# Modulation rows by matmuls of diagonals, and the second modulation part moved to the unit without PV

## The chip, the cores and the metric

The kernel runs on one core of a Trainium2 chip. A core has five engines, each with its own instruction queue: TensorE (PE, with its weight loads shown as PEld), VectorE (DVE), ScalarE (ACT), GpSimd (POOL) and SyncE (SP), which here issues nearly all DMAs. Engines wait for each other and for DMAs through semaphores. The metric is the device time of one execution in microseconds, the median of several runs.

## The reference

One transformer block of the adaptive-layernorm kind, in bf16, for 2048 rows x of width 512. From a condition vector c come six modulation vectors of 512 elements, and then an attention part and a gated MLP are applied, each with a layernorm ahead of it and a gate behind it:

```python
mod = (_silu(c) @ w_mod).reshape(c.shape[0], 6, 1, -1)
sa, ca, ga, sb, cb, gb = (mod[:, 0].copy(), ..., mod[:, 5].copy())
h = _layernorm(x, axis=-1) * (1 + ca) + sa
x = x + ga * _A_ref(h, A_k_cache, A_v_cache, A_wq, A_wo)
h = _layernorm(x, axis=-1) * (1 + cb) + sb
x = x + gb * _B_ref(h, B_w_in, B_w_sp, B_b_sp, B_w_out)
```

`_A_ref` is attention with 32 query heads in 8 groups of 4 over cached keys and values (2048 keys, head width 128), with its projections wq and wo. `_B_ref` is the gated MLP: gelu of h @ w_in, a layernorm of one half, a 2048 x 2048 mix over the rows (w_sp, b_sp), the product with the other half, and w_out.

The vectors ga and gb multiply along the width of a row. Where a tile has 128 rows of x on its partitions and the 512 columns along the free axis, ga is needed as a 128 x 512 tile in which every partition holds the same row (`ga_rows`, `gb_rows`). The matmuls that compute the modulation give it the other way: 128 elements on the partitions, four columns (`modc`).

## The kernel before

**Units.** The attention runs in 128 units (`it` in the main loop, `u` for the unit whose scores are computed): 8 groups times 16 tiles of 128 query rows, each unit with the 4 heads of its group. A unit has 8 slots. In each slot PE computes a 128 x 1024 tile of scores into one of two `s_ps` buffers in PSUM (two matmuls of 512 columns, in `qk`), and ACT takes its exponential into SBUF. In the same slot PE does an eighth of the product with the values (PV) of an earlier unit, and what else the schedule puts there. The order of all work is written out by hand (`manual_schedule`): `at(it, slot, fn)` puts a function at the head of a slot, and `fill[it, slot]` one behind PV.

**By columns and by rows.** Units 0 to 7, the last ones, and every third one between work by columns: the scores have the keys on the partitions (line 1030), the exponentials go straight into a tile `pT`, and PV of the unit runs in the next unit (line 1086). Two of three units from unit 8 (`TURN_A = 2 * CT`) on work by rows (line 1011): the scores have the queries on the partitions, ACT sums each row as it goes (line 1018), and each head's 128 x 2048 exponentials are turned by a DMA transpose on SP's queue (`turn_rows`, line 1050) into a stripe of `pT`. Their PV (line 1065) runs 2 or 3 units later (`LAGS = (2, 3, 1)`). Unit 8's PV is in unit 10, unit 9's in unit 12, unit 10's in unit 11, unit 11's in unit 13. So no PV falls into unit 9.

**Tiles for pT.** There are three: `pT0`, `pT1` and `wsp`. `homes` gives each unit the one that has been free longest. `wsp` first holds the second part of the modulation weights (`wmod_b`, 4 x 512 columns, loaded in unit 1), and counts as free from unit CT + 2 = 6.

**Other work in the slots.** The query projection of the next four units (`qproj`, line 947, 16 matmuls of 512 columns, four for each head, copied out of PSUM by DVE at line 958) is spread over the units before; `set_fill` places it, for block 3 two to a slot over unit 9, with the banks `misc` and `o_ps` in turn. The output projection of a unit (`wo_proj`, line 1143, four matmuls in slots 4 to 7) comes three units after its PV, into the banks `misc`; DVE adds it up (lines 1128 to 1136). A bank name has two buffers.

**The modulation.** A part (`mod_part`, line 857) is 16 matmuls with one column each, for 512 elements. sa and ca are computed ahead of unit 0. sb and cb come from `mod_cols_b` at slot 4 of unit 4, ga and gb from `mod_rows` at slot 4 of unit 5. `mod_rows` copies the four columns of each into `modc`, writes them from POOL's queue into a line in DRAM (line 1216), and reads the line back to all partitions (line 1217). POOL's queue holds the two pairs one behind the other, and the second of each pair waits for the first to land.

**Loads of group 1.** wq, v and wo of group 1 are issued on SP's queue in slot 2 of unit 6 and in slots 2 and 5 of unit 7 (lines 722, 730, 740). `ga_rows` is first used in the last group, `gb_rows` in the last stage.

Of the kernel before, what the change touches and what calls it, by code (L numbers as in the profile page):

```python
# [575 lines left out]
def kernel(  # L576
# [19 lines left out]
    nc = tc.nc  # L596
    _, S, D = A_x.shape
    _, HKV, SK, DH = A_k_cache.shape
    HQ = A_wq.shape[1] // DH
    REP = HQ // HKV  # L600
# [5 lines left out]
    NDT = D // P  # L606
# [3 lines left out]
    CT = 512 // P  # L610
    FC = _f_chunk(FH)
    NFHC = FH // FC
    NSLOT = NKT // 2
# [17 lines left out]
    fast = ctx.enter_context(ExitStack())  # L631
# [3 lines left out]
    psum = fast.enter_context(  # L635
        tc.tile_pool(name="psum", bufs=2, space=bass.MemoryType.PSUM)
    )
    dram = fast.enter_context(tc.tile_pool(name="dram", bufs=1, space=bass.MemoryType.DRAM))
    res = fast.enter_context(tc.tile_pool(name="res", bufs=1))
    stat = fast.enter_context(tc.tile_pool(name="stat", bufs=2))  # L640
    wspp = fast.enter_context(tc.tile_pool(name="wspp", bufs=1, side="right"))
# [6 lines left out]
    ga_rows = res.tile([P, D], FP32, name="ga_rows")  # L648
    gb_rows = res.tile([P, D], FP32, name="gb_rows")
    modc = res.tile([P, 6 * NDT], FP32, name="modc")  # L650
# [12 lines left out]
    wmod_b = wspp.tile([P, NDT * 4 * D], BF16, name="wsp")[:].rearrange(  # L663
        "p (k n) -> p k n", k=NDT
    )
    ident = res.tile([P, P], BF16, name="ident")
    ones_bf = res.tile([P, P], BF16, name="ones_bf")
    mean_bf = res.tile([P, P], BF16, name="mean_bf")

    def bank(name):  # L670
        return psum.tile([P, 512], FP32, name=name)
# [33 lines left out]
    for i in range(2):  # L705
        part = slice(i * D, (i + 1) * D)
# [13 lines left out]
    def load_wq(g, engine):  # L720
        wqs[g] = early.tile([P, NDT, REP * DH], BF16, name="wq_g")
        engine.dma_start(
            out=wqs[g][:], in_=wq_dram[:, :, g * REP * DH : (g + 1) * REP * DH]
        )

    def load_v(g):
        v1 = late.tile([P, NKT, DV], BF16, name="v1")
        nc.gpsimd.memset(v1[:, :, DH:DV], 1.0)
        if g > 0:
            nc.sync.dma_start(out=v1[:, :, 0:DH], in_=v_dram[:, g])  # L730
        else:
            nc.sync.dma_start(out=v1[:, 0 : NKT // 2, 0:DH], in_=v_rows)
            nc.sync.dma_start(
                out=v1[:, NKT // 2 : NKT, 0:DH], in_=v_dram[:, 0, NKT // 2 : NKT]
            )
        groups.setdefault(g, {})["v1"] = v1

    def load_wo(g, engine):
        wo_g = late.tile([P, REP, D], BF16, name="wo_g")
        engine.dma_start(out=wo_g[:], in_=wo_dram[:, g * REP : (g + 1) * REP, :])  # L740
        groups[g]["wo"] = wo_g

    def load_k(g):
        kT = early.tile([P, SK], BF16, name="kT")
        nc.sync.dma_start_transpose(out=kT[:], in_=A_k_cache[0, g])
        groups.setdefault(g, {})["kT"] = kT
# [106 lines left out]
    def mod_part(i, wmod, w0, mc_ps):  # L853

        for dt in range(NDT):
            for kt in range(NDT):
                nc.tensor.matmul(  # L857
                    mc_ps[:, i * NDT + dt : i * NDT + dt + 1],
                    lhsT=wmod[:, kt, w0 + dt * P : w0 + (dt + 1) * P],
                    rhs=sc_bf[:, kt : kt + 1],  # L860
                    start=(kt == 0),
                    stop=(kt == NDT - 1),
                )

    def mod_copy(first, mc_ps):
        c0 = first * NDT
        nc.vector.tensor_copy(out=modc[:, c0 : c0 + NDT], in_=mc_ps[:, 0:NDT])
        nc.vector.tensor_scalar_add(
            out=modc[:, c0 + NDT : c0 + 2 * NDT], in0=mc_ps[:, NDT : 2 * NDT], scalar1=1.0
        )  # L870
# [15 lines left out]
    mc_ps = bank("misc")  # L886
# [15 lines left out]
    for k in range(2):  # L902
        for dt in (2 * k, 2 * k + 1):
# [13 lines left out]
    for dt in range(NDT):  # L917
        if dt == 2:
            k_turn((0, 1, 2, 3), (nc.vector.tensor_copy, nc.scalar.copy))
        for hh in range(REP):  # L920
            nc.tensor.matmul(
                q_ps[hh // 2][:, hh % 2 * P : (hh % 2 + 1) * P],
                lhsT=wqs[0][:, dt, hh * DH : (hh + 1) * DH],
                rhs=hTs[0][:, dt, 0:P],
                start=(dt == 0 and hh % 2 == 0),
                stop=(dt == NDT - 1 and hh % 2 == 1),
            )
    for hf, copy in enumerate((nc.vector.tensor_copy, nc.scalar.copy)):
        copy(
            out=qTs[0][:, 2 * hf : 2 * hf + 2, 0:P],  # L930
            in_=q_ps[hf][:, 0 : 2 * P].rearrange("p (h q) -> p h q", h=2),
# [3 lines left out]
    def qproj(b, heads, c0, n, banks=("misc", "misc")):  # L935

        g, ch = divmod(b, NCH)
        if b not in qTs:
            qTs[b] = early.tile([P, REP, 512], BF16, name="qT")
        one = n * len(heads) <= 512  # L940
        ps = {}

        def mm(hh, dt):
            if dt == 0 and (not one or hh == heads[0]):
                ps[0] = bank(banks[hh % 2])
            o0 = (hh - heads[0]) * n if one else 0
            nc.tensor.matmul(  # L947
                ps[0][:, o0 : o0 + n],
                lhsT=wqs[g][:, dt, hh * DH : (hh + 1) * DH],
                rhs=hTs[ch][:, dt, c0 : c0 + n],  # L950
                start=(dt == 0),
                stop=(dt == NDT - 1),
            )
            if dt == NDT - 1 and (not one or hh == heads[-1]):
                hs = heads if one else [hh]
                dst = qTs[b][:, hs[0] : hs[-1] + 1, c0 : c0 + n]
                src = ps[0][:, 0 : len(hs) * n].rearrange("p (h q) -> p h q", q=n)
                nc.vector.tensor_copy(out=dst, in_=src)  # L958

        return [lambda hh=hh, dt=dt: mm(hh, dt) for hh in heads for dt in range(NDT)]  # L960
# [7 lines left out]
    TURN_A, TURN_B = 2 * CT, NU - CT * 2 - 1  # L968
# [12 lines left out]
        return pv_at(u) + (3 if u < NU - 6 else 2)  # L981


    users, homes = dict(pT0=-2, pT1=-1, wsp=CT + 2), {}
    for u in range(NU):
        homes[u] = min(users, key=lambda k: users[k])
        assert users[homes[u]] < u
# [5 lines left out]
    def at(it, slot, fn):  # L993
        later.setdefault((it, slot), []).append(fn)
# [203 lines left out]
        at(it + 1, 4 if j >= NT - CT else 5, second)  # L1198
        at(it + 2, 5, third)

    def mod_cols_b():
        mc_ps = bank("misc")
        for i in range(2):
            mod_part(i, wmod_b, (1 + i) * D, mc_ps)
        mod_copy(3, mc_ps)

    def mod_rows():

        mc_ps = bank("misc")
        for i, row in enumerate((0, 3)):  # L1210
            mod_part(i, wmod_b, row * D, mc_ps)
        for i, (part, rows) in enumerate(((2, ga_rows), (5, gb_rows))):
            cols = slice(part * NDT, (part + 1) * NDT)
            nc.vector.tensor_copy(out=modc[:, cols], in_=mc_ps[:, i * NDT : (i + 1) * NDT])
            line = dram.tile([D], FP32, name=f"mod{part}")
            nc.gpsimd.dma_start(out=line[:].rearrange("(dt p) -> p dt", p=P), in_=modc[:, cols])
            nc.gpsimd.dma_start(out=rows[:], in_=line[:].partition_broadcast(P))

    def load_wsp(tile_, t, st):
        nc.sync.dma_start_transpose(  # L1220
# [4 lines left out]
    wsp = [None] * NCH  # L1225
# [34 lines left out]
    ln1_at(3, (5, 1), (5, 5), (7, 4))  # L1260
    at(1, 4, lambda: nc.sync.dma_start(out=wmod_b, in_=wmod_dram[:, :, 2 * D : NMOD]))
    at(TURN_B + 1, 2, lambda: nc.sync.dma_start(out=win_sb, in_=win_dram))
    at(4, 4, mod_cols_b)
    at(5, 4, mod_rows)

    def set_fill(b):


        hole = TURN_A + 1 if (TURN_A + 1) // CT == b - 1 else None
        fs = qproj(b, list(range(REP)), 0, 512, ("misc", "o_ps" if hole else "misc"))  # L1270
        for k, fn in enumerate(fs):
            it, slot = (b - 1) * CT + k // NDT, k % NDT
            if hole:
                it, slot = divmod(hole * NSLOT + k // 2 - 1, NSLOT)
            if b == 1:
                it, slot = 2 + (10 + k) // 16, (5 + k // 2) % 8
            elif b == 2:
                it, slot = (5, k // 2) if k < 8 else (it, slot)
            fill.setdefault((it, slot), []).append(fn)
# [8 lines left out]
    for g in range(1, HKV):  # L1288
        it = (g - 1) * NT
        loads = (  # L1290
            (0, lambda g=g: load_wq(g, nc.sync)),
            (4, lambda g=g: load_v(g)),
            (6, lambda g=g: load_wo(g, nc.sync)),
            (8, lambda g=g: load_k(g)),
        )
        last = it - 1
        for from_it, load in loads:
            if g == 1 and from_it < 8:
                at(6 + from_it // 4, 2 + 3 * (from_it // 2 % 2), load)
                continue  # L1300
            last = next(u for u in pauses if u >= it + from_it and u > last)
            at(last + 1, 1, load)
# [93 lines left out]
    for it in range(NU + 6):  # L1396
        if it < NU:
            if it % CT == 0 and it // CT + 1 < NB:
                set_fill(it // CT + 1)
        elif it == NU:  # L1400
            free_a.close()
            z2p = fast.enter_context(tc.tile_pool(name="z2p", bufs=1))
            zs["z2"] = z2p.tile([P, NT, FH], BF16, name="z2")
# [41 lines left out]
    for f in range(NFT):  # L1445
# [6 lines left out]
        out=ok1[:], in0=rall[:], scalar1=1.0 / SAFE, scalar2=None, op0=ALU.is_ge  # L1452
# [8 lines left out]
        out=bad[:], in0=okm[:], scalar1=-1.0, scalar2=1.0, op0=ALU.mult, op1=ALU.add  # L1461
# [149 lines left out]
```

## Time and profile before

| | |
|---|---|
| median of 3 runs | 1314.78 us (1312.67, 1314.78, 1315.01) |
| the profiled execution | 1312.48 us |
| its span | 1310.7 us |
| PE busy | 1299.7 us, 99% |
| ACT busy | 1112.7 us, 85% |
| DVE busy | 672.8 us, 51% |
| POOL busy | 59.6 us, 5% |
| DMA queue of SP | 741168 packets, 199.55 MB, 84.0% of 16 engines' span |
| unit 8, the first by rows, begins | 83.04 us |
| units 16 to 18 | 151.71 to 177.78 us |

A line such as "10.47, 10.47 (x126)" in a windows answer is the length of the stretch, and then each engine's busy time and number of instructions. In a list of the chain of waits, the columns are start, length, and what the chain stood on. In a timeline the bracket gives the idle time of the engine ahead of an instruction and what ended it. "DMA to landing" is the time from the issue of a DMA to its last semaphore update, smallest, median and largest of those asked for.

### The profile page before, as it was taken

The numbers are of one execution on the slowest core, as the hardware profiler recorded it, in microseconds if no ns is written. First come the engines' busy times: TensorE is split into PE (matmuls) and PEld (weight loads), VectorE is DVE, ScalarE is ACT, GpSimd is POOL, SyncE is SP. The second block draws the span as 40 slices with busy tenths as digits, with TensorE's granted clock in tenths as the row PEclk, the third lists the DMA queues.
The fourth block names the chain that finished last, engine by engine and source line by source line (L and its number), as shares of the span: only waits on it lengthen the run. The fifth ranks groups of instructions, "written<-read, shape, count | busy, mean of one in ns | idle before, by whom it ended". The sixth has DMA issues, their size and how long they took to land.

```text
span 1310.7 us, 22899 instructions
## 1 busy us (share of the span) xinstructions
PE 1299.7 (99%) x8807; PEld 705.4 (54%) x8807; DVE 672.8 (51%) x1730; ACT 1112.7 (85%) x1653; POOL 59.6 (5%) x96
## 2 busy tenths in 40 slices
PE   9999999999999999999999999999999999999998
PEld 5654555555555555555555555555555566644445
DVE  6532545454545454545454544455445657693443
ACT  7889999999999999999999999999999988650000
POOL 1100000000000000000000000000000134210000
PEclk9999999999999999999999999999999999999999
DMA  7399999999999999999999999999999921364300
GB/s 195 92 134 185 177 188 185 189 167 186 193 188 167 192 168 191 182 171 192 183 186 166 194 188 184 174 188 173 183 187 176 165 82 29 57 134 100 77 21 31
DMA packets 744102, 203.86 MB, mean 156 GB/s; under 512 B 728240, under 2 KB 742704, under 8 KB 743984
## 3 DMA queue, kind: packets, MB, share of 16 engines
q1 hardware_dynamic: 741168, 199.55, 84.0%
q10 hardware_dynamic: 2592, 2.23, 0.6%
q8 instruction: 71, 1.16, 0.4%
q0 software_dynamic: 224, 0.53, 0.2%
q14 instruction: 47, 0.39, 0.1%
HBM read 21.89 MB, written 2.10 MB: 18 GB/s over the span
## 4 chain that ended last, share of the span: by engine, by line
PE 98%; ACT 1%; DVE 1%; DMA 0%; issue 0%; SPq 0%; ACTq 0%; DVEq 0%
PE s_ps L1011 20%; PE o_ps L1065 19%; PE o_ps L1086 15%; PE s_ps L1030 14%; PE misc L1143 8%; PE misc L947 8%; PE misc L1478 7%; PE s_ps L1313 2%; PE s_ps L1352 2%; PE o_ps L1511 1%; PE s_ps L1511 0%; DMA wmod_a<-in_w_mod_dram 0%; ACT pT L1037 0%; ACT win_sb L1018 0%; PE misc L857 0%; ACT wmod_a L1018 0%
## 5 line engine op out<-in xcount | busy, mean ns | idle before, releaser
L1037 ACT ACTIVATE pT<-s_ps 128x1024 bf16<-128x1024 f32 x408 | 413.7, 1025 | 32.9 <-PE s_ps L1030 15.2
L1011 PE MATMUL s_ps<-kT,qT 128*128 128x512 bf16 x1184 | 352.1, 379 | 0.0
L1018 ACT ACTIVATE win_sb<-s_ps 128x1024 bf16<-128x1024 f32 x298 | 304.9, 1024 | 3.1 <-ACT pn L1018 0.3
L1086 PEld LDWEIGHTS <-pT 128*128 128x128 bf16 x3264 | 218.5, 98 | 95.8
L1030 PE MATMUL s_ps<-qT,kT 128*128 128x512 bf16 x864 | 256.7, 379 | 1.6 <-ACT pT L1037 1.6
L1086 PE MATMUL o_ps<-v,pT 128*128 128x129 bf16 x3264 | 251.6, 220 | 0.0
L1136 DVE SCALAR_TENSOR_TENSOR xacc<-misc,rall,xacc 128x512 f32<-128x512 f32 x290 | 217.1, 749 | 55.3 <-PE misc L1143 49.0
L1018 ACT ACTIVATE pn<-s_ps 128x1024 bf16<-128x1024 f32 x196 | 200.7, 1025 | 1.6 <-PE s_ps L1011 0.4
L1143 PE MATMUL misc<-wo_g,oT 128*128 128x512 bf16 x512 | 194.0, 379 | 0.6 <-DVE qT L958 0.6
L1065 PEld LDWEIGHTS <-v 128*128 128x128 bf16 x1184 | 115.7, 98 | 141.9 <-issue 2.7
L947 PE MATMUL misc<-hT,wq_g 128*128 128x512 bf16 (+2 forms) x520 | 187.0, 371 | 0.1
L1065 PE MATMUL o_ps<-wsp,v 128*128 128x512 bf16 x592 | 176.1, 379 | 1.8 <-DVE rall L1057 1.8
L1065 PE MATMUL o_ps<-pT,v 128*128 128x512 bf16 x592 | 175.4, 379 | 0.0
L1011 PEld LDWEIGHTS <-qT 128*128 128x128 bf16 x1184 | 115.7, 98 | 104.8 <-issue 1.2
L958 DVE CAST qT<-misc 128x512 bf16<-128x512 f32 x125 | 85.8, 687 | 154.4 <-PE misc L947 154.4
L1054 DVE TENSOR_TENSOR tot<-rs 128x1 f32<-128x1 f32 x296 | 46.3, 156 | 167.4 <-ACT win_sb L1018 111.9
L1030 PEld LDWEIGHTS <-kT 128*128 128x128 bf16 x864 | 83.4, 98 | 88.1 <-issue 4.1
L1478 PE MATMUL misc<-wsp,z 128*128 128x512 bf16 (+2 forms) x560 | 100.5, 336 | 0.0
L1018 ACT ACTIVATE wmod_a<-s_ps 128x1024 bf16<-128x1024 f32 x98 | 100.4, 1025 | 0.0
L1097 DVE RECIPROCAL rall<-o_ps 128x2 f32<-128x2 f32 x108 | 18.1, 168 | 115.2 <-PE o_ps L1086 115.1
L1478 PEld LDWEIGHTS <-z 128*128 128x128 bf16 x560 | 50.5, 98 | 48.4 <-issue 0.2
L947 PEld LDWEIGHTS <-wq_g 128*128 128x128 bf16 x528 | 50.4, 98 | 37.3 <-issue 0.4
(105 smaller groups left out, 795.8 us busy)
## 6 DMA issues: line engine op xcount, KB each, us to landing
wo_g<-in_A_wo_dram SPq DMA_DIRECT2D x8, 512.0 KB, 4.6
wq_g<-in_A_wq_dram SPq DMA_DIRECT2D x7, 512.0 KB, 4.6
v<-in_A_v_cache_dram SPq DMA_DIRECT2D x7, 512.0 KB, 5.0
wsp<-in_w_mod_dram SPq DMA_DIRECT2D x1, 2048.0 KB, 8.7
out_dram<-yout ACTq DMA_DIRECT2D x16, 128.0 KB, 1.7
win_sb<-in_B_w_in_dram SPq DMA_DIRECT2D x1, 1792.0 KB, 7.1
x_sb<-in_A_x_dram SPq DMA_DIRECT2D x3, 512.0 KB, 4.9
wsp<-win_sb SPq DMA_TRANSPOSE x75, 4.8
```

What stands on the lines that cost most here:

```text
L947: nc.tensor.matmul(ps[0][:, o0 : o0 + n], lhsT=wqs[g][:, dt, hh * DH : (hh + 1) * DH], rhs=hTs[ch][:, dt, c0 : c0 + n], start=(dt == 0), s ...
L958: nc.vector.tensor_copy(out=dst, in_=src)
L1011: nc.tensor.matmul(s_ps[:, c * 512 : (c + 1) * 512], lhsT=qTs[b][:, hh, jj * P : (jj + 1) * P], rhs=groups[g]["kT"][:, k0 : k0 + 512], sta ...
L1018: nc.scalar.activation(out=rows_of(u, hh)[:, half * HK : (half + 1) * HK], in_=s_ps[:], func=ACT.Exp, scale=inv_sqrt_dh, accum_out=rsums[u ...
L1030: nc.tensor.matmul(s_ps[:, h * 512 : (h + 1) * 512].rearrange("p (r q) -> p r q", r=REP), lhsT=groups[g]["kT"][:, kt * P : (kt + 1) * P], ...
L1037: nc.scalar.activation(out=pTs[u][:, 2 * i : 2 * i + 2, :], in_=s_ps[:].rearrange("p (k q) -> p k q", k=2), func=ACT.Exp, scale=inv_sqrt_dh,)
L1054: nc.vector.tensor_tensor(out=tot[:], in0=rs[:, 2 * hh : 2 * hh + 1], in1=rs[:, 2 * hh + 1 : 2 * hh + 2], op=ALU.add)
L1065: nc.tensor.matmul(o_pss[u][:], lhsT=groups[g]["v1"][:, kt, 0:DH], rhs=pTs[u][:, kt, :], start=(kt == 0), stop=(kt == NKT - 1),)
L1086: nc.tensor.matmul(o_ps[:, hh % 2, 0 : DH + 1], lhsT=pTs[u][:, kt, hh * P : (hh + 1) * P], rhs=groups[g]["v1"][:, kt, 0 : DH + 1], start=( ...
L1136: nc.vector.scalar_tensor_tensor(out=xa[:], in0=X_ps[:], scalar=scale, in1=xa[:], op0=ALU.mult, op1=ALU.add)
L1143: nc.tensor.matmul(ps[0][:], lhsT=oTs[u][:, hh, :], rhs=groups[g]["wo"][:, hh, :], start=(hh == 0 or each), stop=(hh == REP - 1 or each),)
L1478: nc.tensor.matmul(g_pss[f][:, :n], lhsT=z2[:, st, f * P : (f + 1) * P], rhs=wsp[t][:, st, c0 : c0 + n], start=(st == 0), stop=(st == NT - ...
```

## The change

- The functions `mod_cols_b` and `mod_rows` go, with their four DMAs on POOL and the pool in DRAM. In their place `mod_b_part(k)` runs one modulation part each in slots 1, 3, 5 and 7 of unit 9, into a bank of `o_ps`.
- `mod_diag` makes a 128 x 512 bf16 tile that holds four diagonal blocks: the identity, each row scaled by that partition's element of `modc` (four DVE instructions for ga in slot 4 of unit 12, four for gb in slot 5). `mod_row` multiplies a matrix of ones with it in one matmul of 512 columns, so that every partition gets the whole row, and DVE copies it from PSUM to `ga_rows` or `gb_rows` (slots 6 and 7 of unit 12).
- The query projection of block 3 is spread otherwise: four matmuls in unit 8, eight in unit 9, four in unit 10, one in a slot, all into `misc`.
- The loads of group 1 move: wq to slot 2 of unit 4, v to slot 2 of unit 6, wo to slot 2 of unit 7.
- `wsp` counts as free from TURN_A + 1 = 9. Unit 8 then has pT0 instead of wsp, unit 9 pT1, unit 10 wsp, and the turn of the three tiles is shifted from there on.

```diff
-    users, homes = dict(pT0=-2, pT1=-1, wsp=CT + 2), {}
+    users, homes = dict(pT0=-2, pT1=-1, wsp=TURN_A + 1), {}
...
-    def mod_rows():
-
-        mc_ps = bank("misc")
-        for i, row in enumerate((0, 3)):
-            mod_part(i, wmod_b, row * D, mc_ps)
-        for i, (part, rows) in enumerate(((2, ga_rows), (5, gb_rows))):
-            cols = slice(part * NDT, (part + 1) * NDT)
-            nc.vector.tensor_copy(out=modc[:, cols], in_=mc_ps[:, i * NDT : (i + 1) * NDT])
-            line = dram.tile([D], FP32, name=f"mod{part}")
-            nc.gpsimd.dma_start(out=line[:].rearrange("(dt p) -> p dt", p=P), in_=modc[:, cols])
-            nc.gpsimd.dma_start(out=rows[:], in_=line[:].partition_broadcast(P))
+    mod_b = {}
+
+    def mod_b_part(k):
+        if k % 2 == 0:
+            mod_b["ps"] = bank("o_ps")
+        mc_ps = mod_b["ps"]
+        mod_part(k % 2, wmod_b, (1, 2, 0, 3)[k] * D, mc_ps)
+        if k == 1:
+            mod_copy(3, mc_ps)
+        if k == 3:
+            for i, part in enumerate((2, 5)):
+                cols = slice(part * NDT, (part + 1) * NDT)
+                nc.vector.tensor_copy(out=modc[:, cols], in_=mc_ps[:, i * NDT : (i + 1) * NDT])
+
+    diags = {}
+
+    def mod_diag(part):
+        diags[part] = diag = res.tile([P, D], BF16, name="xn1", bufs=4)
+        for dt in range(NDT):
+            col = part * NDT + dt
+            nc.vector.tensor_scalar(
+                out=diag[:, dt * P : (dt + 1) * P],
+                in0=ident[:],
+                scalar1=modc[:, col : col + 1],
+                scalar2=None,
+                op0=ALU.mult,
+            )
+
+    def mod_row(part, rows):
+        r_ps = bank("misc")
+        nc.tensor.matmul(r_ps[:], lhsT=ones_bf[:], rhs=diags[part][:], start=True, stop=True)
+        nc.vector.tensor_copy(out=rows[:], in_=r_ps[:])
...
-    at(4, 4, mod_cols_b)
-    at(5, 4, mod_rows)
+    for k in range(4):
+        at(TURN_A + 1, 2 * k + 1, lambda k=k: mod_b_part(k))
+    for k, (part, rows) in enumerate(((2, ga_rows), (5, gb_rows))):
+        at(TURN_A + 4, 4 + k, lambda part=part: mod_diag(part))
+        at(TURN_A + 4, 6 + k, lambda part=part, rows=rows: mod_row(part, rows))
...
-        fs = qproj(b, list(range(REP)), 0, 512, ("misc", "o_ps" if hole else "misc"))
+        fs = qproj(b, list(range(REP)), 0, 512)
...
-                it, slot = divmod(hole * NSLOT + k // 2 - 1, NSLOT)
+                if k < NDT:
+                    it, slot = hole - 1, k
+                elif k < 3 * NDT:
+                    it, slot = hole, k - NDT
+                else:
+                    it, slot = hole + 1, k - 3 * NDT
...
-                at(6 + from_it // 4, 2 + 3 * (from_it // 2 % 2), load)
+                at(4 + from_it // 2, 2, load)
```

More of the change, by code (lines that the diff above doesn't have):

```diff
@@ L637 @@
     )
-    dram = fast.enter_context(tc.tile_pool(name="dram", bufs=1, space=bass.MemoryType.DRAM))
     res = fast.enter_context(tc.tile_pool(name="res", bufs=1))
@@ L1199, in ln2 @@
         at(it + 2, 5, third)
-    def mod_cols_b():
-        mc_ps = bank("misc")
-        for i in range(2):
-            mod_part(i, wmod_b, (1 + i) * D, mc_ps)
-        mod_copy(3, mc_ps)
-    def mod_rows():
-        mc_ps = bank("misc")
-        for i, row in enumerate((0, 3)):
-            mod_part(i, wmod_b, row * D, mc_ps)
-        for i, (part, rows) in enumerate(((2, ga_rows), (5, gb_rows))):
-            cols = slice(part * NDT, (part + 1) * NDT)
-            nc.vector.tensor_copy(out=modc[:, cols], in_=mc_ps[:, i * NDT : (i + 1) * NDT])
-            line = dram.tile([D], FP32, name=f"mod{part}")
-            nc.gpsimd.dma_start(out=line[:].rearrange("(dt p) -> p dt", p=P), in_=modc[:, cols])
-            nc.gpsimd.dma_start(out=rows[:], in_=line[:].partition_broadcast(P))
+    mod_b = {}
[26 more added lines that the diff above has]
+        nc.vector.tensor_copy(out=rows[:], in_=r_ps[:])
     def load_wsp(tile_, t, st):
```

## The prediction

> **What bounds the kernel now.** I read the page first, then the chain of waits, then windows cut at the units' starts, then the DMAs that land in the early units.
>
> ```profile
> span 1310.7 us, 22899 instructions
> PE 1299.7 (99%) x8807; PEld 705.4 (54%) x8807; DVE 672.8 (51%) x1730; ACT 1112.7 (85%) x1653; POOL 59.6 (5%) x96
> ```
>
> PE is the bound, and its idle time is only 1310.7 - 1299.7 = 11.0 us. So an edit is worth what it takes from PE's work, and what it fills of PE's few stalls. The units (one unit is one turn of the main loop) lie like this; columns: busy time of PE, PEld, DVE, ACT, POOL, granted clock, DMA share, GB/s.
>
> ```profile
> 44.66:53.46 8.80, 8.80 (x118) 6.43 (x116) 2.92 (x11) 8.04 (x9) 0.00 (x0) 1.00 0.10 19
> 53.46:63.93 10.47, 10.47 (x126) 7.17 (x124) 7.62 (x21) 8.19 (x9) 2.32 (x3) 1.00 0.22 40
> 63.93:74.24 10.31, 8.97 (x90) 5.97 (x88) 2.38 (x6) 7.85 (x9) 1.33 (x2) 1.00 1.03 95
> 83.04:91.52 8.48, 8.48 (x87) 5.77 (x85) 3.00 (x12) 8.40 (x16) 0.77 (x2) 1.00 1.08 159
> 91.52:99.42 7.90, 7.90 (x36) 3.38 (x35) 4.45 (x15) 7.48 (x17) 0.00 (x0) 1.00 1.17 229
> 99.42:108.24 8.82, 7.88 (x36) 3.37 (x36) 1.02 (x4) 8.05 (x10) 0.00 (x0) 1.00 1.04 196
> 116.45:124.62 8.17, 8.17 (x37) 3.51 (x36) 2.98 (x12) 8.16 (x17) 0.00 (x0) 1.00 1.08 210
> 124.62:134.43 9.81, 8.95 (x42) 3.94 (x41) 4.13 (x8) 8.62 (x10) 0.00 (x0) 1.00 1.17 180
> 151.71:177.78 26.07, 26.07 (x169) 13.78 (x168) 13.10 (x35) 25.58 (x41) 0.00 (x0) 1.00 0.98 171
> ```
>
> These are units 4 to 6, 8 to 10, 12, 13, and then 16 to 18 as the steady state, which is PE without a gap. Units 4 and 5 have no PE gap either. Unit 6 has a gap of 10.31 - 8.97 = 1.34, units 10 and 13 have 0.94 and 0.86. Unit 9 is the unit without PV.
>
> **The two modulation parts in units 4 and 5.** The chain has them on PE:
>
> ```profile
> 48.26 0.78 PE misc L857 x32
> 58.73 0.78 PE misc L857 x32
> ```
>
> 64 matmuls cost 1.56 us where PE is the bound. Taken out there, they save all of it.
>
> **Unit 9 and its neighbours.** What PE needs for units 8 to 13, from the chain's pieces:
>
> ```profile
> 83.04 0.43 PE s_ps L1011 x2
> 83.47 0.45 PE o_ps L1086 x8
> 98.12 1.09 ACT win_sb L1018 x4
> 100.88 0.59 PE o_ps L1065 x2
> 101.90 0.43 PE o_ps L1065 x2
> ```
>
> 48 score slots at 0.43, 24 slots of PV by rows at 0.43, 16 by columns at 0.45, and 20 output and 24 query matmuls at 0.216 (half of the 0.43 for two): 20.64 + 10.32 + 7.20 + 4.32 + 5.18 = 47.66 us. They took 134.43 - 83.04 = 51.39. So 3.73 us are lost there: 0.94 + 0.86 are the two gaps, and the rest are slots stretched by ACT, which is the chain from 98.12 on. ACT takes just under 1.0 us a slot by rows:
>
> ```profile
> 84.53 1.02 ACT L1018 ACTIVATE win_sb<-s_ps 128x1024 bf16<-128x1024 f32 x1
> 85.52 1.02 ACT L1018 ACTIVATE win_sb<-s_ps 128x1024 bf16<-128x1024 f32 x1
> ```
>
> That is 0.99, or 8.0 a unit. Unit 9 had 16 + 14 + 4 wide matmuls, 7.3 us: the hole is already nearly full, and ACT's 8.0 sets it. After the change it has 16 + 8 + 4 wide ones (6.05) and the 64 small ones (1.56): 7.6, still below 8.0. Four query matmuls go to unit 8 (two were there) and four to unit 10, which add 0.43 and 0.86 where PE has slots to catch up in.
>
> **The way through DRAM.** Its four POOL DMAs go. What they do now:
>
> ```profile
> L1216 POOL DMA_DIRECT2D mod<-modc x2: 767/910/1052, 60.0 to 72.2; - x2
> DMA to landing us min/median/max: 4.4/6.0/11.3
> 71.67 0.57 POOL L1217 DMA_DIRECT2D ga_rows<-mod  x1 [10.61 <-issue]
> 83.84 0.55 POOL L1217 DMA_DIRECT2D gb_rows<-mod  x1 [10.83 <-DMA mod<-modc]
> ```
>
> Each 2 KB write of single elements takes over 10.6 us, and the second starts at 72.24. While they run, others land late: the same four transposes into hT, issued at 38.1 to 42.9 and at 60.1 to 64.4, and the load of v.
>
> ```profile
> L847 SPq DMA_TRANSPOSE hT<-xn x4: 1217/1223/2046, 38.1 to 42.9; - x4
> DMA to landing us min/median/max: 2.4/2.5/3.2
> L847 SPq DMA_TRANSPOSE hT<-xn x4: 1217/1220/1563, 60.1 to 64.4; - x4
> DMA to landing us min/median/max: 8.5/9.1/9.7
> v<-in_A_v_cache_dram SPq DMA_DIRECT2D x7, 512.0 KB, 5.0
> DMA to landing us min/median/max: 11.6/11.6/11.6
> ```
>
> The last line is v's load at 76.0 alone. 9.1 against 2.5 and 11.6 against 5.0: nothing lands until the write does. PE's gap in unit 6 follows a pause of ACT that ends in the same moment:
>
> ```profile
> 70.37 0.59 PE L1030 MATMUL s_ps<-qT,kT 128*128 128x512 bf16 x2
> 71.90 8.23 ACT L1037 ACTIVATE pT<-s_ps 128x1024 bf16<-128x1024 f32 x8 [2.07 <-PE s_ps L1030]
> ```
>
> ACT was free for 2.07 us with scores from the matmuls before 70.37 in PSUM, and started 0.23 us after POOL was let go at 71.67. No data wait explains that; I put it down to the same hold-up. The second write and the 256 KB broadcast at 83.84 push the first transposes of unit 8:
>
> ```profile
> 76.88 4.07 SPq L740 DMA_DIRECT2D wo_g<-in_A_wo_dram  x1
> 85.85 9.96 SPq L1050 DMA_TRANSPOSE wsp<-win_sb  x3
> 95.91 2.11 SPq L1050 DMA_TRANSPOSE wsp<-wmod_a  x1
> DMA to landing us min/median/max: 4.4/4.7/7.5
> ```
>
> The fourth goes at 95.91 and lands 4.7 later, at 100.6; PV of unit 8 starts at 100.88. So the gap of unit 10 is this landing, not the DVE instruction that the profile names. PE is through unit 8 at 91.52 and ACT about a slot later, so this head could have gone some 3 us earlier. SP's lateness is handed on to unit 11's stripes and the gap of unit 13.
>
> The Trainium skill (DMA: Bandwidth & Descriptors, Anatomy of one DMA — SWDGE (gpsimd) path) puts such a DMA at about 2.0 us plus bytes over 436 GB/s, so 2.0 us for 2 KB. The trace has 11.3. By that rule the write would be done at 62 and could not be what holds ACT at 71; this is the rival "held by something else" below.
>
> **Part by part.** (1) 64 small matmuls leave units 4 and 5: -1.56. (2) No writes, no hold-up of ACT in unit 6: -1.34. (3) Units 8 to 13 need 47.66 + 1.56 + 0.43 (two row matmuls at 0.216) = 49.65. If the stripes land in time, what is left of the stalls is unit 9's 8.0 - 7.6 = 0.4, and about 0.3 at the bank hand-over: the third head's and the output's matmuls in slot 4 of unit 9 now share two banks, and one must wait for a query copy of 0.68 begun at the end of slot 3, while PE brings 0.65 of other work. So 50.35 for 51.39: -1.04. Sum -3.94.
>
> ```profile
> L958 DVE CAST qT<-misc 128x512 bf16<-128x512 f32 x18 | 12.3, 682 | 12.4 <-PE misc L947 12.4
> L816 DVE TENSOR_SCALAR hT<-misc,modc 128x128 bf16<-128x128 bf16 x4 | 1.2, 332 | 0.1
> ```
>
> (4) DVE: eight scalings of a 128x128 block, at most 0.33 (these read SBUF, the row reads PSUM), and two copies out of PSUM of the width of the CAST row, 0.68 each: 4.0 us in unit 12, where DVE works 2.98 of 8.17. It fits, and the row matmuls come two slots (2.0 us) after their four scalings (1.3). A row matmul that waits holds PE's score matmuls of its slot, and so ACT; a copy that waits for it (0.4) holds the next row sums, which only the output step of later units needs. Uncovered this would cost up to 4.0; I take 0, as every row lies under its cover. (5) SP: group 1's wq, v and wo loads move to units 4, 6 and 7. wq's issue leaves 66.99 for about 47, where DMA share is 0.10; nothing is queued close behind it. v passes to about 67, and wo keeps its place but finds the queues free, so its 4.07 shrinks. Their users come in unit 12 and later: 0. (6) POOL: its issues and waits from 60.0 to 83.84 go; behind them stood only a memset for v's ones, used in unit 17: 0. (7) The pT homes: only units 8 to 10 have one unit of slack in place of two, as all later ones have: 0. After unit 13 PE sets everything as before.
>
> **The rivals.** (a) *Held by something else*: ACT's pause and the late stripes stay, moved along with PE. Then units 8 to 13 keep their 51.39, in whose lost 3.73 the added 1.56 + 0.43 disappear, and only (1) is gained: about -1.5. For it: no row shows the write holding ACT. Against: the landings of 9.1 and 11.6 in just these stretches.
> (b) *The hole is full*: the pause goes and the stripes are in time, but the small matmuls at the head of slots 1, 3, 5 and 7 starve ACT (a slot gets 0.39 more, 1.04 to 1.25 against ACT's 1.0), and 1.56 come back: about -2.4. Against it: slots 0, 2, 4, 6 have 0.65 to 0.86.
> (c) *Slower, by the banks*: the query heads in units 8 to 10 lose the o_ps bank and share two misc banks with the output. At five hand-overs PE would wait for a query copy (0.68), an accumulation of the same width (also 0.68, an estimate) and a scaling's worth of what stands between them in DVE's order (0.33). At the full price 5 x 1.69 - 3.9 = 4.5 slower; it decides from 3.9 / 5 = 0.8 a hand-over. Against it, the same sharing in all other units:
>
> ```profile
> L947 PE MATMUL misc<-hT,wq_g 128*128 128x512 bf16 (+2 forms) x520 | 187.0, 371 | 0.1
> L1143 PE MATMUL misc<-wo_g,oT 128*128 128x512 bf16 x512 | 194.0, 379 | 0.6 <-DVE qT L958 0.6
> ```
>
> 0.7 us of waiting in over a thousand matmuls.
>
> **The numbers.** The profiled execution took 1312.48 (span 1310.7 and 1.8 around it); the three runs are 1312.67, 1314.78 and 1315.01, so it stands 2.3 below their median and by the fastest. -3.9 gives 1308.6 against it and 1310.9 against the median. As I can't tell which the changed kernel's median will be nearer to, I take the middle, 1309.7 (its own range 1307.8 to 1311.2: all 4.6 us of stalls gone, to the median's figure with 0.3 less). (a) gives 1312.1, (b) 1311.2, (c) 1318.1, each in that middle frame. Chances: forecast 0.60, (a) 0.17, (b) 0.15, (c) 0.08. What can be told from no change is 0.2%, 2.6 us: the forecast is beyond it, (a) and most of (b) within, (c) beyond on the other side. A part of the forecast's case may fall short of 2.6, a part of (b) may pass it: faster 0.66, same 0.26, slower 0.08. The range takes in (a) against the median (1313.3) and the forecast with all stalls gone against the profiled execution (1307.8), and leaves out (c): 1307.3 to 1313.6.
>
> **What would show it.** Right: hT's last four transposes land in some 2.5 us, ACT has no gap near 70, unit 8's fourth transpose goes within a microsecond or two of its ACT, PV of units 8 and 11 starts without a PE gap, PE's idle time falls by about 3, and the steady state begins about 4 us earlier. Wrong: PE gaps on L857 or the row matmul's line, waits for DVE in units 8 to 10, an ACT pause in unit 6 all the same, or a gap at the end of unit 12.

## The result, and the profile after

The changed kernel takes 1308.36 us (median of 6 runs, 1308.07 to 1308.74) against 1314.41 us before (6 runs, 1312.38 to 1315.12): a ratio of 0.9956, 95% interval 0.9946 to 0.9967. Its profiled execution took 1308.74, 3.74 less than the profiled execution of before; the forecast from that frame was 3.94 less. Before's runs scatter over some 3 us, the changed kernel's over 0.7.

The first lines of the page, as they stood for before:

```profile
span 1306.8 us, 22904 instructions
PE 1298.8 (99%) x8809; PEld 705.7 (54%) x8809; DVE 674.7 (52%) x1740; ACT 1113.5 (85%) x1653; POOL 56.6 (4%) x92
```

PE is idle for 8.0 us in place of 11.0, and its busy time falls by 0.9 though it has two matmuls more. Windows cut at the units' starts (columns: busy time of PE, PEld, DVE, ACT, POOL, granted clock, DMA share, GB/s) for units 4, 5, 6, then 8 to 13, then 16 to 18:

```profile
44.61:52.64 8.03, 8.03 (x88) 5.66 (x85) 2.50 (x9) 7.88 (x9) 0.00 (x0) 1.00 0.38 100
52.64:62.31 9.67, 9.67 (x94) 6.36 (x92) 7.32 (x20) 8.19 (x9) 1.42 (x3) 1.00 0.20 40
62.31:71.11 8.80, 8.80 (x89) 5.97 (x88) 2.38 (x7) 8.19 (x9) 0.00 (x0) 1.00 0.55 108
79.92:88.73 8.81, 8.81 (x90) 5.98 (x88) 3.26 (x13) 8.73 (x16) 0.00 (x0) 1.00 0.69 127
88.73:96.83 8.10, 7.90 (x93) 4.31 (x92) 3.44 (x17) 8.09 (x17) 0.00 (x0) 1.00 1.06 179
96.83:105.46 8.63, 8.63 (x41) 3.92 (x40) 2.21 (x6) 8.34 (x10) 0.00 (x0) 1.00 1.13 212
105.46:113.67 8.21, 8.21 (x85) 5.67 (x84) 2.86 (x11) 8.15 (x16) 0.00 (x0) 1.00 1.13 163
113.67:121.87 8.20, 8.20 (x39) 3.72 (x38) 5.35 (x22) 8.19 (x17) 0.00 (x0) 1.00 1.05 185
121.87:130.51 8.64, 8.64 (x42) 3.92 (x40) 4.01 (x9) 8.35 (x10) 0.00 (x0) 1.00 1.15 192
147.90:173.97 26.07, 26.07 (x169) 13.79 (x168) 13.10 (x34) 25.58 (x41) 0.00 (x0) 1.00 0.98 170
```

The starts of units 4 to 14 are here those of the timeline. The list of the chain puts the same matmuls 0.16 us later (unit 8 of before at 83.04, where the timeline has 82.88), and some windows ahead of this section mix the two. Before, by the timeline's starts, units 8 to 11 and unit 13 are:

```profile
82.88:91.52 8.64, 8.64 (x87) 5.87 (x86) 3.16 (x13) 8.56 (x16) 0.77 (x2) 1.00 1.07 156
91.52:99.35 7.83, 7.83 (x36) 3.31 (x34) 4.44 (x14) 7.41 (x17) 0.00 (x0) 1.00 1.17 230
99.35:108.24 8.89, 7.95 (x37) 3.44 (x36) 1.03 (x4) 8.12 (x10) 0.00 (x0) 1.00 1.04 196
108.24:116.45 8.21, 8.21 (x86) 5.68 (x84) 2.86 (x11) 8.15 (x16) 0.00 (x0) 1.00 1.22 175
124.62:134.27 9.65, 8.79 (x41) 3.85 (x40) 3.98 (x8) 8.46 (x10) 0.00 (x0) 1.00 1.17 179
```

Against the same units before, unit 4 is shorter by 0.77, unit 5 by 0.80, unit 6 by 1.50, unit 10 by 0.26 and unit 13 by 1.01; unit 8 is longer by 0.17, unit 9 by 0.27, unit 12 by 0.03. Units 16 to 18 take the same 26.07. Unit 8 begins 2.96 us earlier (79.92 for 82.88) and unit 14 3.76 earlier (130.51 for 134.27), which is the whole gain.

ScalarE's timeline over unit 6, and then the last four transposes into hT and the load of v in that stretch (a line of the group, and the landing times of each tile):

```profile
59.64 20.84 ACT L1036 ACTIVATE pT<-s_ps 128x1024 bf16<-128x1024 f32 x19
```

```profile
L846 SPq DMA_TRANSPOSE hT<-xn x4: 1190/1216/1217, 59.2 to 63.2; - x4
DMA to landing us min/median/max: 2.4/2.4/4.6
```

```profile
DMA to landing us min/median/max: 4.4/4.4/4.4
```

ACT runs 19 exponentials without a pause, where there was one of 2.07 us. The transposes land in 2.4 us where they took 9.1, v in 4.4 where it took 11.6. SyncE's timeline in units 8 and 9, and pieces of the chain at PV of unit 8, the two row matmuls, and PV of unit 11:

```profile
82.80 6.89 SPq L1049 DMA_TRANSPOSE pT<-win_sb  x3
89.78 3.47 SPq L1049 DMA_TRANSPOSE pT<-wmod_a  x1
```

```profile
96.99 0.43 PE s_ps L1029 x2
97.42 0.43 PE o_ps L1064 x2
...
119.88 0.22 PE misc L1230
...
120.96 0.21 PE misc L1230
...
122.04 0.43 PE s_ps L1029 x2
122.47 0.43 PE o_ps L1064 x2
```

The fourth stripe of unit 8 goes at 89.78 in place of 95.91, and PV of both units follows the scores at once. Neither row matmul has a gap ahead of it.

### The profile page after: what moved, and what is told of

The parts are those of the page before. It is cut to its first block, busy times and chain, and to the rows that moved or that the text cites. A ratio compares the mean times of both kernels' runs of the same rounds, so it can differ in the third digit from the quotient of the medians.

```text
span 1306.8 us, 22904 instructions
## 1 busy us (share of the span) xinstructions
PE 1298.8 (99%) x8809; PEld 705.7 (54%) x8809; DVE 674.7 (52%) x1740; ACT 1113.5 (85%) x1653; POOL 56.6 (4%) x92
## 4 chain that ended last, share of the span: by engine, by line
PE 92%; DVE 0%; issue 0%
PE o_ps L1064 20%; PE s_ps L1010 19%; PE o_ps L1085 13%; PE s_ps L1029 12%; PE misc L1142 8%; PE misc L946 8%; PE misc L1500 7%; PE s_ps L1335 2%; PE s_ps L1374 2%; PE o_ps L1533 1%; PE s_ps L1533 0%; PE o_ps L856 0%; DVE xacc L1135 0%; DVE tmp L1545 0%; DVE bnst L697 0%; DVE qT L957 0%
## 5 line engine op out<-in xcount | busy, mean ns | idle before, releaser
L1036 ACT ACTIVATE pT<-s_ps 128x1024 bf16<-128x1024 f32 x256 | 258.8, 1026 | 16.8 <-PE s_ps L1029 4.8
L1064 PE MATMUL o_ps<-pT,v 128*128 128x512 bf16 x896 | 265.8, 379 | 0.0
L1036 ACT ACTIVATE wsp<-s_ps 128x1024 bf16<-128x1024 f32 x176 | 179.5, 1024 | 13.4 <-PE s_ps L1029 5.6
L946 PE MATMUL misc<-hT,wq_g 128*128 128x512 bf16 (+2 forms) x528 | 190.7, 371 | 0.1
L1085 PEld LDWEIGHTS <-pT 128*128 128x128 bf16 x2048 | 136.8, 98 | 59.0
L1085 PE MATMUL o_ps<-v,pT 128*128 128x129 bf16 x2048 | 157.2, 220 | 0.0
L1085 PEld LDWEIGHTS <-wsp 128*128 128x128 bf16 x1408 | 94.3, 98 | 41.5
L1085 PE MATMUL o_ps<-v,wsp 128*128 128x129 bf16 x1408 | 108.5, 220 | 0.0
L1064 PE MATMUL o_ps<-wsp,v 128*128 128x512 bf16 x288 | 85.7, 379 | 0.0
```

The lines of the kernel that those rows point to most:

```text
L946: nc.tensor.matmul(ps[0][:, o0 : o0 + n], lhsT=wqs[g][:, dt, hh * DH : (hh + 1) * DH], rhs=hTs[ch][:, dt, c0 : c0 + n], start=(dt == 0), s ...
L1036: nc.scalar.activation(out=pTs[u][:, 2 * i : 2 * i + 2, :], in_=s_ps[:].rearrange("p (k q) -> p k q", k=2), func=ACT.Exp, scale=inv_sqrt_dh,)
L1064: nc.tensor.matmul(o_pss[u][:], lhsT=groups[g]["v1"][:, kt, 0:DH], rhs=pTs[u][:, kt, :], start=(kt == 0), stop=(kt == NKT - 1),)
L1085: nc.tensor.matmul(o_ps[:, hh % 2, 0 : DH + 1], lhsT=pTs[u][:, kt, hh * P : (hh + 1) * P], rhs=groups[g]["v1"][:, kt, 0 : DH + 1], start=( ...
```

## The experiments

**The diagonals alone.** Kernel before, with only the way through DRAM replaced. The modulation parts stay in units 4 and 5; query projection, loads and pT tiles stay as they were (`mod_diag` and `mod_row` are those of the change).

```diff
-            line = dram.tile([D], FP32, name=f"mod{part}")
-            nc.gpsimd.dma_start(out=line[:].rearrange("(dt p) -> p dt", p=P), in_=modc[:, cols])
-            nc.gpsimd.dma_start(out=rows[:], in_=line[:].partition_broadcast(P))
...
+    for k, (part, rows) in enumerate(((2, ga_rows), (5, gb_rows))):
+        at(TURN_A + 4, 4 + k, lambda part=part: mod_diag(part))
+        at(TURN_A + 4, 6 + k, lambda part=part, rows=rows: mod_row(part, rows))
```

> The kernel before with one part of the change alone: the modulation parts stay in units 4 and 5, the query projection and the loads stay, and only the way through DRAM is replaced by the diagonals and the row matmuls in unit 12. Theory (the single-element writes to DRAM hold up other DMAs, ACT's pause in unit 6 and the late transposes come from them): no pause in unit 6 (1.34 us of PE), no landing over 5 us in units 5 to 8, the PE gaps of units 10 and 13 gone, and 0.43 us of new matmuls; units 8 to 13 are then set by ACT rather than PE, so about 3.2 us less than the kernel before at its fastest, 1309.3. Rival (held by something else, for instance wq's load and the transposes themselves): the pause and the landings of 8 us and more stay, and the time is that of before, plus 0 to 0.4.

Measured: 1308.98 (1308.54 to 1309.28) against 1314.06 in the same batch, ratio 0.9963 (0.9949 to 0.9976). So the DRAM way alone is worth nearly all of the gain. Units 8 to 13 as one window, first of before, then of this kernel, then of the changed one:

```profile
83.04:134.43 51.39, 49.59 (x318) 25.65 (x316) 18.44 (x58) 48.88 (x81) 0.77 (x2) 1.00 1.13 191
```

```profile
81.38:131.02 49.64, 49.59 (x320) 25.93 (x319) 20.82 (x69) 48.67 (x81) 0.00 (x0) 1.00 1.02 179
```

```profile
79.92:130.51 50.59, 50.39 (x384) 27.52 (x382) 21.13 (x73) 49.85 (x81) 0.00 (x0) 1.00 1.03 176
```

PE's 1.80 us of idle time in before's window is down to 0.05. The rest of the change, above all the small matmuls and the wider spread of the query projection, then adds 0.95, and ACT is at work for 49.85 of 50.59 us.

**Only the move.** The changed kernel with the way through DRAM put back, from the end of unit 9 on.

```diff
+                line = dram.tile([D], FP32, name=f"mod{part}")
+                nc.gpsimd.dma_start(out=line[:].rearrange("(dt p) -> p dt", p=P), in_=modc[:, cols])
+                nc.gpsimd.dma_start(
+                    out=(ga_rows, gb_rows)[i][:], in_=line[:].partition_broadcast(P)
+                )
...
-    for k, (part, rows) in enumerate(((2, ga_rows), (5, gb_rows))):
-        at(TURN_A + 4, 4 + k, lambda part=part: mod_diag(part))
-        at(TURN_A + 4, 6 + k, lambda part=part, rows=rows: mod_row(part, rows))
```

> The changed kernel with the way through DRAM put back: parts in unit 9, homes, loads and query projection as changed, and the two writes and two broadcasts on POOL's queue from the end of unit 9. Theory: the writes now fall on units 10 to 12, each holding up landings for about 9 us, where the stripes of units 9 and 11 are awaited; PE gaps of 3 to 8 us there, 1311 to 1316. Rival (held by something else): about the changed kernel's 1308.4, less 0.4 for the two row matmuls that it lacks.

Measured: 1325.84 (1325.05 to 1327.66), ratio 1.0094 (1.0078 to 1.0109): the right direction, and 10 us beyond the top of what was expected. The landing times of the two writes and two reads, one wait, and two 10-us windows of this kernel:

```profile
DMA to landing us min/median/max: 4.5/8.6/15.9
```

```profile
PEld L1065 <- DMA pT<-win_sb: 12.4, 1, 12.4
```

```profile
120.00:130.00 10.00, 4.18 (x14) 1.64 (x15) 0.33 (x2) 1.58 (x3) 0.55 (x1) 0.57 1.18 97
...
140.00:150.00 10.00, 10.00 (x54) 4.80 (x53) 4.29 (x6) 8.02 (x10) 0.00 (x0) 0.89 1.04 174
```

One write took 15.9 us to land here, where unit after unit hangs on its stripes, and PV waited 12.4 us for one. The granted clock fell too: 0.57 in 120 to 130, when PE stood idle for much of the time, and still 0.89 in 140 to 150, when it was busy throughout. So this stall cost more than itself: 0.89 over ten busy microseconds is about 1.1 us, an estimate.

**One write, later.** The changed kernel and one 2 KB write more. It was put at unit 60, but nothing holds POOL to the slots: it went out at 444.7 us.

```diff
+    def lone_write():
+        line = dram.tile([D], FP32, name="lone")
+        nc.gpsimd.dma_start(out=line[:].rearrange("(dt p) -> p dt", p=P), in_=modc[:, 2 * NDT : 3 * NDT])
+
+    at(60, 4, lone_write)
```

> The changed kernel plus one write of 2 KB in single elements from POOL to DRAM in unit 60, in the steady state; nobody reads it. Theory: it lands 9 to 11 us after its issue, no other DMA lands in between, and PE, which waits for a unit's stripes that come some 2 us ahead, stands for 4 to 8 us there: 1312 to 1316. By the 2.0 us that the skill's formula gives for such a DMA: no PE gap, 1308.4.

Measured: 1309.97 (1309.76 to 1311.22), which is 1.4 to 1.6 above the changed kernel's two medians (1308.36, 1308.54): seen, and smaller than expected. The write's landing, that of the stripes into pT in 444 to 465 us, and PE's one gap there:

```profile
DMA to landing us min/median/max: 10.1/10.1/10.1
...
DMA to landing us min/median/max: 4.4/5.9/9.0
```

```profile
463.69 0.59 PE L1065 MATMUL o_ps<-pT,v 128*128 128x512 bf16 x2 [1.48 <-DMA pT<-win_sb]
```

The stripes land in up to 9.0 us (5.1 at most in the changed kernel's same stretch), and PE waits 1.48 for one. ACT makes no pause of its own here: its one long gap, 1.70 us ahead of 464.96, comes behind PE's.

**The same write in longer runs.** As the last, with `"(p dt) -> p dt"` in place of `"(dt p) -> p dt"`: 128 runs of 16 bytes in place of 512 of 4, the same 2 KB.

> The kernel of e3 with the same lone write of the same 2 KB, laid out so that each partition writes one run of 16 bytes instead of four runs of 4 bytes: 128 pieces instead of 512. If the time goes by the pieces: a landing in about 10.1 / 4 = 2.5 to 4 us, no PE gap, and the changed kernel's 1308.4. If it is the write from POOL's queue whatever its pieces: a landing of 10 us and a PE gap of 1.5 as in e3, 1310.0.

Measured: 1308.45 (1307.96 to 1308.66), no cost. Landing of the write, and of the stripes in 444 to 465 us:

```profile
DMA to landing us min/median/max: 3.1/3.1/3.1
...
DMA to landing us min/median/max: 4.4/4.8/5.1
```

The pieces make the price, not the bytes: 384 pieces fewer take 7.0 us off the landing, 18 ns a piece. (The pair also changes where the pieces lie in DRAM; no run separates the two.) The Trainium skill (DMA: Bandwidth & Descriptors, Anatomy of one DMA — SWDGE (gpsimd) path) has the same 2.0 us for both forms, since its rule goes by bytes; the 3.1 is not far from it, the 10.1 is. The same page (Rules for kernel authors) says that a last dimension which is not contiguous becomes one descriptor per element and is to be rearranged; this pair of runs agrees.

**One read.** The changed kernel and one 256 KB broadcast read from POOL's queue in unit 8, as the one from the line in DRAM was; what it reads is overwritten later.

```diff
+    def lone_read():
+        nc.vector.memset(gb_rows[:, 0:1], 0.0)
+        nc.gpsimd.dma_start(
+            out=gb_rows[:].bitcast(BF16), in_=B_b_sp[0 : 2 * D].partition_broadcast(P)
+        )
+
+    at(8, 2, lone_read)
```

> The changed kernel plus one broadcast of 2 KB from DRAM to all 128 partitions (256 KB) on POOL's queue at slot 2 of unit 8, about where the second broadcast of the kernel before stood; its data is overwritten later. If the broadcast is a good part of what delayed the first transposes of unit 8: the first one's issue takes 4 to 5 us instead of 2, the fourth is issued 2 to 3 us later, with a small PE gap or none, 1308.4 to 1309.4. If the writes alone did it: nothing to see, 1308.4.

Measured: 1308.34 (1307.96 to 1309.02), no cost. Its landing, and SyncE's next stripes:

```profile
DMA to landing us min/median/max: 3.9/3.9/3.9
```

```profile
82.79 8.61 SPq L1049 DMA_TRANSPOSE pT<-win_sb  x3
91.49 2.59 SPq L1049 DMA_TRANSPOSE pT<-wmod_a  x1
```

It puts the fourth stripe off by 1.7 us (91.49 for 89.78), which PV at 97.4 doesn't feel.

**One write where before had its first.** The kernel with the diagonals alone, and `lone_write` (512 pieces) in slot 5 of unit 5 or, in a second kernel, of unit 4; a third has it in slot 1 of unit 6.

```diff
+    at(5, 5, lone_write)
```

> The kernel of e1 (the kernel before with the diagonals alone) plus one write of 2 KB in single elements from POOL, in the place of the first write of the kernel before (unit 5, about 60 us); nothing reads it and there is no broadcast. If the pause of ACT in unit 6 comes with the write: a pause of about 2 us near 70, PE's gap of 1.3 there, landings into hT of 8 to 10 us, no gap in units 10 and 13, and 1309.0 + 1.3 = 1310.3. If the pause needs the broadcast that follows, or something else that e1 changed: no pause, 1309.0, with the late landings all the same.

> As e5, with the write at unit 4, about 50 us, ten microseconds earlier. If the pause follows the write at a fixed distance: a pause near 60, some 10 us after the issue, and about 1310.3. If it belongs to what PE and ACT do near 70: none, or one near 70, whatever the write does. Fewer transposes are under way there (one into oT), so few late landings to be seen.

> As the run with the lone write in unit 5 (diagonals alone, and one write of 512 elements of 4 bytes), but the write goes out some 4 us later, in slot 1 of unit 6. There the pause of ScalarE began at 69.6 and ended at 71.5, 11.7 us after the write. Theory A: the pause hangs on the write's landing and moves with it: it ends near 75 to 76, and its start moves too. Theory B: it hangs on a place in the program near 70 at which something cannot get past the write: it begins at 69.6 again and ends with the write, so it is 5 to 6 us long and the time is 1311 to 1314. Theory C: no pause at all, since nothing that the engines need falls into the write's 11 us: 1309.1 as with the write in unit 4.

Measured: 1309.82 (1309.36 to 1310.24) with the write in unit 5 and 1309.12 (1308.48 to 1309.56) in unit 4, in one batch. ScalarE's timeline after the write, and the landing of the last four transposes into hT, for unit 5 (write issued at 59.8):

```profile
71.53 11.53 ACT L1037 ACTIVATE pT<-s_ps 128x1024 bf16<-128x1024 f32 x11 [1.94 <-PE s_ps L1030]
```

```profile
DMA to landing us min/median/max: 8.7/9.3/9.8
```

and for unit 4 (issued at 49.5):

```profile
59.99 21.94 ACT L1037 ACTIVATE pT<-s_ps 128x1024 bf16<-128x1024 f32 x20 [1.09 <-PE s_ps L1030]
```

```profile
DMA to landing us min/median/max: 2.4/2.7/3.6
```

One write at 60 brings back both the pause of unit 6 and the late transposes, without the second write and without the reads; ten microseconds earlier it brings no pause. That the transposes are in time there says little: they are issued from 60.1 on, more than ten microseconds behind that write. The packets show what is late. On SyncE's queue between 64 and 66 us there ran, first with the write in unit 5, then in the changed kernel:

```profile
q1 hardware_dynamic: 1028, 0.25, 61.1%
q1 hardware_dynamic: 777, 0.19, 47.8%
```

So at this time the transposes' data moves while the write is under way, and not more slowly; what comes late is the landing, the semaphore update behind the data. Later, between 69 and 70 us, no packet begins on any queue in the four profiles with the pause (in the changed kernel 1014 do, with the diagonals alone 332), and ACT's pause begins in the same microsecond (69.5 to 70.0). The Trainium skill (DMA: Bandwidth & Descriptors, Queues, rings and completion order) says that each DMA engine turns from queue to queue after every packet. The trace agrees in so far as these 1028 packets ran during the write, but it did not help the landings: where they took 2.4 to 3.6 us they took 8.7 to 9.8.

The third kernel missed its aim. POOL again ran ahead of the slots, and its write went out at 60.1:

```profile
L1287 POOL DMA_DIRECT2D lone<-modc x1: 976/976/976, 60.1 to 60.1; - x1
```

```profile
71.67 11.53 ACT L1037 ACTIVATE pT<-s_ps 128x1024 bf16<-128x1024 f32 x11 [1.72 <-PE s_ps L1030]
```

So it is a repeat: a pause again, ending 11.5 us after the write, at 1310.39 (1310.22 to 1311.37). Whether the pause moves with a later write is not settled.

**Kernel before, once more.**

> The kernel before, unchanged, for a second profile. Its runs lie in two groups, 1312.4 to 1312.7 and 1314.1 to 1315.1. Theory: the hold-up by the writes differs from run to run, so a run in the upper group has a longer pause or larger PE gaps in units 6 to 13, by 2.3 us in sum. Rival: the two groups come from elsewhere, and the early units are as in the first profile.

Measured: 1313.10, with the pause again (ACT idle for 2.00, to 71.47) and the gaps of units 10 and 13 behind late stripes. The chain of waits in this execution names the transposes themselves:

```profile
96.99 4.71 DMA wsp<-wmod_a
...
122.20 4.34 DMA wsp<-pn
```

Its time is 0.6 above that of the first profile, and the late stripes more than account for it: units 8 to 13 take 52.4 us in place of 51.4, and PE's gap ahead of PV of unit 8 is 1.93 in place of 0.94.

```profile
101.83 0.59 PE L1065 MATMUL o_ps<-wsp,v 128*128 128x512 bf16 x2 [1.93 <-DMA wsp<-wmod_a]
```

The upper runs of before, 1314 and more, did not come under the profiler.

**The modulation parts back.** The changed kernel with the parts in units 4 and 5 (and their bank `misc` again), all else as changed.

```diff
-            mod_b["ps"] = bank("o_ps")
+            mod_b["ps"] = bank("misc")
...
-    for k in range(4):
-        at(TURN_A + 1, 2 * k + 1, lambda k=k: mod_b_part(k))
+    at(4, 4, lambda: [mod_b_part(k) for k in (0, 1)])
+    at(5, 4, lambda: [mod_b_part(k) for k in (2, 3)])
```

> The changed kernel with the 64 small modulation matmuls put back into units 4 and 5 and all else as changed: step 1 of the prediction alone, turned back. Units 4 and 5 must get 2 x 0.78 = 1.56 us longer. What units 8 to 13 give back tells which limit they have in the changed kernel. Theory A (as the prediction's sum has it, the matmuls bound them): they get 1.56 shorter and the time is that of the changed kernel, 1308.4 within 0.3. Theory B (they are held by the exponentials as much as by the matmuls, as the run with the diagonals alone suggests): they give back about 1.0 and the time is 1309.0, up to 0.9 more than the changed kernel. Rival: they give nothing back, 1309.9.

> The changed kernel again, beside the others on one chip: 1308.4 within 0.3. Its last four transposes of the normalised rows land in 2.4 us and ScalarE has no pause near 70, as in its first profile; if one of the two fails, the write was not the only cause of the delays there.

Measured in one batch: 1309.77 (1309.6 to 1311.5) with the parts back, 1308.54 (1308.15 to 1308.82) for the changed kernel, whose second profile again has no pause and transposes of 2.4 us. So the move is worth 1.23, near the rival's 1.5 (nothing given back) and twice theory B's 0.6. Units 8 to 13 with the parts back:

```profile
81.17:131.47 50.30, 49.61 (x320) 25.90 (x319) 20.76 (x69) 49.57 (x81) 0.00 (x0) 1.00 1.04 178
```

64 matmuls fewer make these units only 0.29 shorter than the changed kernel's 50.59, nearly all of it in unit 9, which takes 7.83 (89.97 to 97.80) in place of 8.10. There PE then waits for ACT three times, 0.69 us together:

```profile
91.77 0.59 PE L1010 MATMUL s_ps<-kT,qT 128*128 128x512 bf16 x2 [0.29 <-ACT pn L1017]
92.77 0.59 PE L1010 MATMUL s_ps<-kT,qT 128*128 128x512 bf16 x2 [0.20 <-ACT pn L1017]
93.78 0.59 PE L1010 MATMUL s_ps<-kT,qT 128*128 128x512 bf16 x2 [0.20 <-ACT pn L1017]
```

In the changed kernel one such gap of 0.20 is left. So 1.56 us of matmuls cost 0.27 in unit 9: it was the right place for them.

**The loads back.** The changed kernel with group 1's loads in units 6 and 7.

```diff
-                at(4 + from_it // 2, 2, load)
+                at(6 + from_it // 4, 2 + 3 * (from_it // 2 % 2), load)
```

> The changed kernel with the four loads of group 1 put back to units 6 and 7 where they were: step 5 of the prediction alone, turned back. Theory: the loads lie on SyncE with two units to spare in either place and the time is that of the changed kernel, 1308.4 within 0.2. Rival: the places were chosen because in units 6 and 7 they delay the transposes behind them, which would cost 0.5 to 1.5 us: 1308.9 to 1309.9, and a gap of TensorE in units 8 to 10 would show.

Measured: 1308.51 (1308.26 to 1308.77) beside 1308.54: nothing.

No kernel tried is faster than the changed one by more than its scatter.

## Why the prediction was right

The sum of -3.94 against the profiled execution met -3.74; the steps (1) to (3) measure -3.87 in sum, and the changed kernel's unit 4 begins 0.11 later. Step by step:

- **(1) Small matmuls out of units 4 and 5, -1.56.** Measured -0.77 and -0.80, so -1.57. That row counts of small matmuls can be taken at full price where PE is the bound held to the hundredth.
- **(2) No pause in unit 6, -1.34.** Measured -1.50. The gap was read 0.16 too small: the profile counts it from the recorded end of the last matmul, 0.38 after its start, and these matmuls start 0.22 apart. The cause, argued from two moments that fell together, holds as far as this: with the write at 60 there is a pause (both profiles of before, and two kernels with one write alone), without it there is none. What ACT waits for in it no record shows. All that its instruction needed from PE was there, and the write in the middle of the kernel made no such pause. That DMA packets stop at the same time, from 69 to 70 us, is a trail and not a cause shown.
- **(3) Units 8 to 13, -1.04.** Measured -0.80, 50.59 for the forecast 50.35. The mechanism was right: stripes in time, no gap at PV of units 8 and 11. The term that was mis-sized is what stays of the stalls: 0.7 forecast, and 50.59 - 49.65 = 0.94 measured. It also lies elsewhere. At the forecast's own prices unit 9 has 0.5 of it (8.10 for 7.6; 0.4 was forecast) and unit 11 has 0.3 (8.21 for 7.9), which the forecast left out, though unit 11 took 8.21 before as well. The 0.3 at a bank hand-over doesn't show: in slot 4 of unit 9 PE has no gap ahead of a query or output matmul. So that 0.7 came near 0.94 was in part luck. The two units are those whose matmuls need less than ACT's 8.0; the others take what their matmuls need, within 0.04.
- **Why the parts don't add.** With the diagonals alone the counted work of units 8 to 13 is 48.09 (47.66 + 0.43) and the stretch takes 49.64, so 1.55 are lost with hardly a gap on record, slots stretched by ACT as in before. The rest of the change adds 1.56 of matmuls there and 0.95 of time, since added matmuls partly fill such slots: 0.27 of it comes in unit 9, and 0.17 and 0.51 in units 8 and 10, which get two and four query matmuls more (unit 8 takes 8.64 and unit 10 8.12 with the diagonals alone). So the diagonals alone bring 3.25 of the 3.76 (unit 14 at 131.02), and the move, 1.56 by count, brings 0.51 more in the profiles (131.02 to 130.51), though with the other edits in place taking it back costs 1.23.
- **(4) DVE, (5) loads, (7) pT tiles: 0.** The row matmuls have no gap, and unit 12 grows by 0.03 for two of 0.22. The loads were tried alone: nothing. The tiles were not tried alone; no gap answers to them.
- **(6) POOL: 0.** Nothing of POOL's stands in the chain after.
- **The rivals.** (a) falls by the diagonals alone, and by the single write. (b) would have unit 9 held up by the small matmuls; it took 8.10, with one gap of 0.20, where the forecast had 8.0, and 7.83 without them. (c) has nothing for it: PE's waits at the output matmuls are 0.6 us in all, as before.

What was off is the frame. I set the figure at 1309.7, midway between 1308.6 (from the profiled execution) and 1310.9 (from the median). The first was the right one. The changed kernel's medians stayed at 1308.4 and 1308.5, while before's were 1314.41, 1314.06, 1311.66 and 1313.67 in four batches, with single runs from 1309.72 to 1317.41. In the batch of 1311.66 the changed kernel itself did not run; with the one read added, which cost nothing, it took 1308.34. So the gain is 3.3 to 6.1 us by the batch. The two profiles of before, 0.6 apart, differ by how badly the hold-up hits units 8 to 13, and that the whole scatter comes from it is likely, not shown: what the upper runs of before lose beyond these two profiles stays open. If it does, subtracting a fixed gain from the median kept a part of the loss that the change removes.

## What to carry to other kernels

A tiny DMA can be the dearest in the kernel: look at how long each takes to land, and at which others land late in that time; write longer runs (16 bytes sufficed here), or turn a vector by a matmul of ones with a diagonal, at 0.22 us of PE and some scalings on an engine with room. Where two engines are both nearly full, the gains of single edits need not add up, so try each alone and each taken out. And a kernel whose runs scatter more than those of its variants may have something in it that is hit by chance; in this one case, when it went, reckoning from the lowest times was right.

## What was not expected of the hardware

- A write of 512 pieces of 4 bytes, 2 KB, landed in 10.1 to 15.9 us and held back the landings of other DMAs of the core for as long (transposes 9.3 us for 2.4), while their packets ran on for most of it; in 128 pieces of 16 bytes it landed in 3.1 and held back nothing.
- ScalarE stood still for 1.7 to 2.1 us, until 11.5 to 11.9 us after the issue of such a write, in each of four profiles with the write at 60, with nothing in the records for it to wait on.
- Around a stall in which PE stood idle for 11.9 us the granted clock was 0.57 over ten microseconds, and still 0.89 over ten in which PE was busy again.
